# The first four token tiles loaded in two halves, the planner's tie rule and starting times for VectorE and GpSimd changed, and a new order of operations

## The chip, the core and the metric

The kernel runs on one core of a Trainium2 chip. A time is the device time of one execution in microseconds (us). Three executions of the kernel before took 198.56, 198.58 and 199.02 us; their median, 198.58 us, is the time that the change is measured against.

## The reference

A transformer block on x of 2048 tokens by 512 channels, all in bf16, with one conditioning vector c (512) that gives six modulation vectors. The first half is linear attention with 32 heads of 16 channels; the second is a gated feed-forward network with 1376 hidden units.

```python
mod = (_silu(c) @ w_mod)                       # sa, ca, ga, sb, cb, gb
h = _layernorm(x) * (1 + ca) + sa
q, k, v = split(h @ wqkv)                      # 32 heads of 16
pq, pk = q @ w_phi, k @ w_phi                  # per head
phi = concat(softmax(p), softmax(-p))          # for q and for k
kv, z = phi_k^T v, sum(phi_k)
o = (phi_q kv) / (phi_q z + 1e-6)
x = x + ga * (o @ wo)
h = _layernorm(x) * (1 + cb) + sb
x = x + gb * ((silu(h @ w_gate) * (h @ w_up)) @ w_down)
```

## The kernel before, in words

Tokens are worked on in 16 tiles of 128; four tiles are a chunk (`x_c0` to `x_c3` in the rows). Every weight is loaded into SBUF once. The work of a tile goes in this order. First the layer norm: VectorE takes statistics (`st`, `ln_mv`), ScalarE or GpSimd forms the reciprocal deviation, one of three engines writes the normalised tile `xn`. Then `xn` is turned (by TensorE for the first tiles, by a transposing DMA into `raw` for the later ones) and modulated into `hT`. TensorE multiplies it into keys (line 705), values (709) and queries (803). ScalarE takes exponentials (`e`, `eq`), VectorE sums them (`S`, `Sq`), and GpSimd or VectorE scales half of them (lines 774 and 827). The products of keys and values are summed over all tiles in the PSUM tile `kv_ps` (line 780). After the sixteenth tile VectorE makes `KVZ` from it. Then each query tile, turned into `pT` by a DMA, is multiplied with it (line 951), divided into `o`, turned into `oT`, multiplied with `wo` (line 984) and added to x. A second layer norm follows, then gate and up products (line 1044, and line 1090 for the last 96 hidden units), silu on ScalarE, a product on VectorE or GpSimd (`gu`), and the down projection (line 1122).

Before any key can be computed the program prepares two weights. `w_phi` (`wphi_sb`) becomes a block matrix `BD` (16 short matmuls in line 571, then GpSimd). The key weight `wk` is turned by TensorE (16 transposes in line 600 into four PSUM banks), copied to `WT512` (line 604), multiplied with `BD` (line 611, four matmuls a bank) and cast back into `wk` (line 614). Between these stand the products of c with `w_mod` (line 547), whose result `modA` is needed for the first `hT` (line 652).

The order of all operations is written out as a table. `ORDER` holds some 940 numbers: a number divided by four names an operation, the remainder chooses the engine among its alternatives. Each engine's queue is that list with the other engines' operations left out, so the order on each engine and the buffers that an operation gets come from `ORDER` alone. The planner's `run` walks these queues with a table of costs. Its times decide two things only: in what order the operations are written into the program, and how many filler matmuls (line 1196: products of a constant tile with itself, whose result nobody uses) `fill` puts in front of a TensorE operation that the plan expects to start late. Filler was put in ahead of the first key matmul only. An operation with the mark `DVE*` is a VectorE operation from SBUF to SBUF; the plan lets such an operation and a GpSimd operation exclude each other in time. `Buf(at=...)` tells the plan from when a loaded buffer may be read. Where two candidates may start at the same time, the plan takes the one for which the second value is smaller:

```python
if best is None or (t, not o.star) < best[:2]:
    best = t, not o.star, o
```

All transposing DMAs and nearly all loads and stores are issued by SyncE (SP) in the order of the table, each waiting there until what it reads is ready.

Of the kernel before, what the change touches and what calls it, by code (L numbers as in the profile page):

```python
# [20 lines left out]
D = 512  # L21
KD = D // P
# [13 lines left out]
def fm_size(m):  # L36
# [84 lines left out]
class Plan:  # L121
# [67 lines left out]
    def run(self, fill):  # L189
# [4 lines left out]
        for _ in self.ops:  # L194
            best = None
            for e, q in queue.items():
                if head[e] == len(q):
                    continue
                o = q[head[e]]
# [10 lines left out]
                if best is None or (t, not o.star) < best[:2]:  # L210
                    best = t, not o.star, o
# [33 lines left out]
def kernel(  # L245
# [128 lines left out]


    bx = [Buf() for _ in range(NT)]
    bwk, bwv, bwq = [Buf()] * KD, Buf(), [Buf()] * KD
    bm1, bm2 = [Buf() for _ in range(KD)], [Buf(), Buf()]
    bwo = [Buf() for _ in range(KD)]
    bwd = [Buf() for _ in range(FM)]  # L380
# [855 lines left out]
```

## Time and profile before

| | us |
|---|---|
| median of three executions | 198.58 |
| the profiled execution | 198.82 |
| its span, first to last instruction | 197.0 |
| TensorE busy in the span | 189.3 |
| VectorE busy | 131.6 |
| ScalarE busy | 114.2 |
| GpSimd busy | 113.4 |

The profiled execution is 0.24 us above the median; 1.82 us of it lie outside the span. TensorE is busy for 96% of the span, in every slice of the page except the first and the last with at least eight tenths. Busy time of TensorE includes filler and matmuls at the lower clock, so the share alone does not say what is left to gain.

### The profile page before, as it was taken

The numbers are of one execution on the slowest core, as the hardware profiler recorded it, in microseconds if no ns is written. First come the engines' busy times: TensorE is split into PE (matmuls) and PEld (weight loads), VectorE is DVE, ScalarE is ACT, GpSimd is POOL, SyncE is SP. The second block draws the span as 40 slices with busy tenths as digits, with TensorE's granted clock in tenths as the row PEclk, the third lists the DMA queues.
The fourth block names the chain that finished last, engine by engine and source line by source line (L and its number), as shares of the span: only waits on it lengthen the run. The fifth ranks groups of instructions, "written<-read, shape, count | busy, mean of one in ns | idle before, by whom it ended". The sixth has DMA issues, their size and how long they took to land.

```text
span 197.0 us, 3999 instructions
## 1 busy us (share of the span) xinstructions
PE 189.3 (96%) x1455; PEld 107.3 (54%) x1479; DVE 131.6 (67%) x262; ACT 114.2 (58%) x259; POOL 113.4 (58%) x184
## 2 busy tenths in 40 slices
PE   5989999999999999999999999999999999999993
PEld 2755555544655867977655455444444444454442
DVE  4899999999999989989857636531322620242453
ACT  2699999998899973873962775542322325430000
POOL 1658999999696976765581736745204424240510
DMA  5998994999948894937976431210000010100222
GB/s 195 389 372 117 170 344 129 223 391 232 278 118 156 77 195 78 161 68 113 191 92 131 84 80 46 61 36 0 13 3 13 0 53 0 53 5 13 80 82 67
DMA packets 51142, 24.17 MB, mean 123 GB/s; under 512 B 42449, under 2 KB 47922, under 8 KB 51122
## 3 DMA queue, kind: packets, MB, share of 16 engines
q1 hardware_dynamic: 50832, 23.86, 51.3%
q8 instruction: 11, 0.18, 0.4%
q10 hardware_dynamic: 290, 0.05, 0.1%
q14 instruction: 9, 0.07, 0.1%
HBM read 11.58 MB, written 2.10 MB: 69 GB/s over the span
## 4 chain that ended last, share of the span: by engine, by line
PE 83%; DVE 6%; POOL 4%; DMA 3%; issue 2%; DVEq 0%; POOLq 0%
PE one_ps L1044 34%; PE one_ps L1122 17%; PE one_ps L984 7%; PE one_ps L803 6%; PE one_ps L705 4%; PE one_ps L709 4%; PE one_ps L1090 3%; DVE st L404 2%; DMA wphi_sb<-in_A_w_phi_dram 2%; PE kv_ps L951 2%; PE kv_ps L780 2%; POOL e L774 2%; POOL xn L473 2%; DVE Sq L811 1%; DMA out_dram<-ot 1%
## 5 line engine op out<-in xcount | busy, mean ns | idle before, releaser
L1044 PE MATMUL one_ps<-hT,wgu_sb 128*128 128x512 bf16 (+2 forms) x475 | 73.6, 307 | 0.3
L1044 PEld LDWEIGHTS <-wgu_sb 128*128 128x128 bf16 x480 | 40.4, 98 | 28.9
L1060 POOL TENSOR_TENSOR gu<-usb,sg 128x512 bf16<-128x512 bf16 x19 | 21.9, 1155 | 36.2 <-ACT usb L1058 18.8
L1051 ACT ACTIVATE sg<-one_ps 128x512 bf16<-128x512 f32 (+1 forms) x41 | 23.2, 588 | 30.4 <-PE one_ps L1044 25.9
L1122 PE MATMUL one_ps<-wd_sb,gu 128*128 128x512 bf16 (+1 forms) x155 | 37.2, 372 | 0.2
L1054 DVE TENSOR_TENSOR gu<-one_ps,sg 128x512 bf16<-128x512 f32 (+1 forms) x22 | 14.2, 654 | 19.7 <-PE one_ps L1044 13.9
L1132 DVE TENSOR_TENSOR fg<-one_ps,gab 128x512 bf16<-128x512 f32 (+1 forms) x16 | 10.6, 669 | 24.2 <-PE one_ps L1122 24.2
L1122 PEld LDWEIGHTS <-gu 128*128 128x128 bf16 x180 | 16.7, 98 | 17.2
L811 DVE TENSOR_REDUCE Sq<-eq 128x64 f32<-128x1024 bf16 x16 | 19.3, 1208 | 0.0
L728 DVE TENSOR_REDUCE S<-e 128x64 f32<-128x1024 bf16 x16 | 18.6, 1207 | 0.2 <-ACT e L720 0.2
L720 ACT ACTIVATE e<-one_ps 128x512 bf16<-128x512 f32 x32 | 16.8, 603 | 0.9 <-PE one_ps L705 0.9
L807 ACT ACTIVATE eq<-one_ps 128x512 bf16<-128x512 f32 x32 | 16.9, 603 | 0.7 <-PE one_ps L803 0.5
L1058 ACT CAST usb<-one_ps 128x512 bf16<-128x512 f32 x19 | 11.0, 584 | 9.7 <-PE one_ps L1044 8.3
L984 PE MATMUL one_ps<-wo_sb,oT 128*128 128x512 bf16 x58 | 15.2, 379 | 0.6 <-DVE gul L1097 0.3
L705 PE MATMUL one_ps<-wk,hT 128*128 128x512 bf16 x62 | 15.0, 379 | 0.7 <-ACT hT L652 0.6
L803 PE MATMUL one_ps<-wq,hT 128*128 128x512 bf16 x63 | 15.4, 379 | 0.1
L709 PE MATMUL one_ps<-wv,hT 128*128 128x512 bf16 x60 | 15.2, 379 | 0.1
L774 POOL TENSOR_TENSOR e<-e,rho 128x512 bf16<-128x512 bf16 x14 | 14.5, 1050 | 0.2
L995 DVE SCALAR_TENSOR_TENSOR x_c<-one_ps,x_c 128x512 bf16<-128x512 f32 x14 | 9.4, 679 | 6.1 <-PE one_ps L984 6.0
L827 POOL TENSOR_TENSOR eq<-eq,Rq 128x512 bf16<-128x512 bf16 x12 | 12.5, 1048 | 0.5
L404 DVE BATCH_NORM_STATS2 st<-x_c 128x6 f32<-128x512 bf16 x17 | 11.0, 679 | 1.8 <-DMA x_c<-in_A_x_dram 1.8
L998 ACT ACTIVATE xn<-x_c 128x512 bf16<-128x512 bf16 x14 | 8.7, 627 | 5.9 <-DMA raw<-xn 3.2
(138 smaller groups left out, 274.1 us busy)
## 6 DMA issues: line engine op xcount, KB each, us to landing
wmod_sb<-in_w_mod_dram SPq DMA_DIRECT2D x2, 1024.0 KB, 7.3
out_dram<-ot SPq DMA_DIRECT2D x15, 128.0 KB, 1.9
x_c<-in_A_x_dram SPq DMA_DIRECT2D x3, 512.0 KB, 6.7
wgu_sb<-in_B_w_up_dram SPq DMA_DIRECT2D x1, 1376.0 KB, 7.2
wgu_sb<-in_B_w_gate_dram SPq DMA_DIRECT2D x1, 1376.0 KB, 12.0
wd_sb<-in_B_w_down_dram SPq DMA_DIRECT2D x1, 1280.0 KB, 7.2
wk<-in_A_wqkv_dram SPq DMA_DIRECT2D x1, 512.0 KB, 4.7
wmod_sb<-in_w_mod_dram SPq DMA_DIRECT2D x1, 512.0 KB, 6.0
```

Of the source, the lines that this page charges most:

```text
L705: nc.tensor.matmul(pk()[:], lhsT=hT[c_i][k][:, cols], rhs=Wk2[:, k, :], start=(k == 0), stop=(k == KD - 1))
L709: nc.tensor.matmul(v()[:], lhsT=hT[c_i][k][:, cols], rhs=wv_sb[:, k, :], start=(k == 0), stop=(k == KD - 1))
L728: pl.op("DVE", r=[e], w=([Ss] if y == 0 else []) + [parts[y]], us=1.13, fn=lambda: nc.vector.tensor_reduce(Ss()[:, y].rearrange("p g (s h) ...
L774: eng.tensor_tensor(e()[:, :, 1], e()[:, :, 1], rho()[:, y].unsqueeze(2).to_broadcast([P, G, DH, 4]), op=ALU.mult)
L803: nc.tensor.matmul(pq()[:], lhsT=hT[c_i][k][:, cols], rhs=Wq2[:, k, :], start=(k == 0), stop=(k == KD - 1))
L807: pl.op("ACT", r=[pq, btab], w=[be[sg]], us=0.48, fn=lambda sg=sg: nc.scalar.activation(eq[:, :, sg].rearrange("p g f h -> p g (f h)"), pq ...
L811: pl.op("DVE", r=be, w=[Sq], us=1.13, fn=lambda: nc.vector.tensor_reduce(Sq()[:].rearrange("p g s h -> p (g s) h"), eq[:].rearrange("p g s ...
L984: nc.tensor.matmul(a()[:], lhsT=oT()[:, j0 + j, :], rhs=wo_sb[:, j, :], start=(j == 0), stop=(j == KD - 1))
L1044: nc.tensor.matmul(ps_()[0:fsz, q * n:(q + 1) * n], lhsT=wgu_sb[:, k, i, m * P:m * P + fsz], rhs=h2[k], start=(k == 0), stop=(k == KD - 1))
L1051: pl.op("ACT", r=[g, btab], w=[sg], us=0.08 + 0.41 * L / CW, fn=lambda: nc.scalar.activation(sg()[0:fsz, 0:L], g()[0:fsz, 0:L], ACT.Silu))
L1060: pl.op("POOL", r=[usb, sg], w=[gu], us=0.17 + 0.98 * L / CW, fn=lambda: nc.gpsimd.tensor_tensor(gu()[0:fsz, 0:L], usb()[0:fsz, 0:L], sg() ...
L1122: nc.tensor.matmul(fp()[:], lhsT=b()[0:fsz, c0:c0 + P], rhs=wd_[0:fsz, m, wcs], start=(m == 0), stop=(m == FM - 1))
```

## The change

The first four tiles of x are loaded in two transfers of two tiles (256 KB each) instead of one of 512 KB. The plan is told that `w_phi` can be read from 4.7 us (3.4 before) and `wk` from 6.3 us (0 before), and that some transfers count for slightly more or fewer bytes. On a tie the plan now takes the engine, VectorE or GpSimd, whose last exclusive operation ended earlier. `ORDER` is a new list. No other line differs; the line numbers of the program after are higher by one or two.

```diff
 ORDER = [
-    0, 4, 72, 56, 60, 65, 80, 8, 12, 76, 85, 128, 120, 132, 124, 88, 94, 44, 48, 52, 216, ...
+    60, 0, 76, 72, 84, 80, 88, 4, 132, 65, 124, 48, 52, 136, 128, 140, 92, 8, 236, 241, 56, ...
...
-                if best is None or (t, not o.star) < best[:2]:
-                    best = t, not o.star, o
+                late = o.star != (pool >= star)
+                if best is None or (t, late) < best[:2]:
+                    best = t, late, o
...
-    bwk, bwv, bwq = [Buf()] * KD, Buf(), [Buf()] * KD
+    bwk, bwv, bwq = [Buf(at=6.3)] * KD, Buf(), [Buf()] * KD
...
-    bc, bphi = Buf(at=5.5), Buf(at=3.4)
+    bc, bphi = Buf(at=5.5), Buf(at=4.7)
...
-    later(x_ch[0][:], x_v[0], bx[0:4], 480)
-    later(Wk2[:], wqkv_v[:, :, D:2 * D], bwk[0:1], 640)
-    for k, n, kb in ((0, 2, 660), (2, 1, 270), (3, 1, 260)):
+    for t in (0, 2):
+        later(x_ch[0][:, t:t + 2, :], x_v[0][:, t:t + 2, :], bx[t:t + 2], 278)
+    later(Wk2[:], wqkv_v[:, :, D:2 * D], bwk[0:1], 556)
+    for k, n, kb in ((0, 2, 665), (2, 1, 252), (3, 1, 256)):
...
-    later(wv_sb[:], wqkv_v[:, :, 2 * D:3 * D], [bwv], 560)
+    later(wv_sb[:], wqkv_v[:, :, 2 * D:3 * D], [bwv], 500)
```

The new table gives some operations to another engine. The counts, before and after, are: scalings of `eq` on VectorE 4 and 1, on GpSimd 12 and 15; second-norm writes of `xn` on VectorE 5 and 1, the others on ScalarE and GpSimd; copies to `WT512` on VectorE 2 and 3, on ScalarE 2 and 1; the small copy of `phs` on ScalarE before and on VectorE after; the first pair's reciprocal deviation on GpSimd before and on ScalarE after. TensorE has the same work in both, apart from filler.

The first place is the head of TensorE's queue. These are its rows in the program before where the filler ends and the 16 short matmuls on `wphi_sb` begin; five fillers of 512 columns stand ahead of them, and three more of 512 follow them.

```order
L1196 LDWEIGHTS ones_101
L1196 MATMUL kv_ps_72<-ones_101 128x512
L571 LDWEIGHTS WT0_98
L571 MATMUL one_ps0_73<-wphi_sb_89,WT0_98 128x16
```

In the program after, the same place reads as below; eight fillers of 512 columns and one of 154 stand ahead of it, and a single one of 449 columns stands between the four short matmuls on `c_row` and the transposes of `wk`.

```order
L1198 MATMUL kv_ps_72<-ones_101 128x512
L1198 LDWEIGHTS ones_101
L1198 MATMUL kv_ps_72<-ones_101 128x154
L573 LDWEIGHTS WT0_98
L573 MATMUL one_ps0_73<-wphi_sb_89,WT0_98 128x16
```

Filler has moved from behind the short matmuls to ahead of them. The two fillers of 512 columns and one of 312 ahead of the first key matmul are in both programs.

The second place is VectorE's queue after the statistics of the first two tiles; `st61` and `st62` are the statistics of the third and fourth. Before:

```order
L404 BN_STATS st62_258<-x_c0_79 128x6
L405 BN_AGGR ln1_mv2_183<-st61_246 128x2
L405 BN_AGGR ln1_mv2_183<-st62_258 128x2
L459 TENSOR_REDUCE ln1_0_nmr_181<-ln1_mv0_179 128x2
L534 TENSOR_TENSOR silucT_136<-sig_134,one_ps1_74 128x4
L467 TENSOR_SCALAR xn0_282<-x_c0_79,ln1_mv0_179,ln1_0_nmr_181 128x512
L604 COPY WT512_186<-one_ps5_78 128x4x128
L604 COPY WT512_186<-one_ps4_77 128x4x128
L459 TENSOR_REDUCE ln1_2_nmr_184<-ln1_mv2_183 128x2
L467 TENSOR_SCALAR xn1_322<-x_c0_79,ln1_mv2_183,ln1_2_nmr_184 128x512 x2
L552 COPY modA_137<-one_ps1_74 128x8
```

And after, from the third tile's statistics on:

```order
L579 COPY phs_143<-one_ps0_73 128x64
L405 BN_STATS st62_255<-x_c0_79 128x6
L406 BN_AGGR ln1_mv2_183<-st61_244 128x2
L406 BN_AGGR ln1_mv2_183<-st62_255 128x2
L460 TENSOR_REDUCE ln1_0_nmr_181<-ln1_mv0_179 128x2
L606 COPY WT512_186<-one_ps2_75 128x4x128
L536 TENSOR_TENSOR silucT_136<-sig_134,one_ps1_74 128x4
L606 COPY WT512_186<-one_ps3_76 128x4x128
L460 TENSOR_REDUCE ln1_2_nmr_184<-ln1_mv2_183 128x2
L606 COPY WT512_186<-one_ps5_78 128x4x128
L468 TENSOR_SCALAR xn1_319<-x_c0_79,ln1_mv2_183,ln1_2_nmr_184 128x512
L468 TENSOR_SCALAR xn0_281<-x_c0_79,ln1_mv0_179,ln1_0_nmr_181 128x512
```

The copies of the turned `wk` now stand ahead of all three writes of `xn`, and there are three of them.

The third place is SP's queue where the attention of the first pairs of tiles is turned: `eq` into `pT` for the query tiles, `o` into `oT` for the product with `wo`. Before:

```order
L831 DMA_TRANSPOSE pT1_857<-eq1_161 128x8x128
L974 DMA_TRANSPOSE oT0_1080<-o0_1050 128x8x128
L831 DMA_TRANSPOSE pT2_918<-eq6_166 128x8x128
L831 DMA_TRANSPOSE pT3_1047<-eq7_167 128x8x128
L831 DMA_TRANSPOSE pT0_841<-eq9_169 128x8x128
L1006 DMA_TRANSPOSE raw0_1332<-xn21_1231 128x8x128
```

After:

```order
L833 DMA_TRANSPOSE pT0_918<-eq1_161 128x8x128
L833 DMA_TRANSPOSE pT2_952<-eq6_166 128x8x128
L833 DMA_TRANSPOSE pT3_1050<-eq7_167 128x8x128
L833 DMA_TRANSPOSE pT1_934<-eq9_169 128x8x128
L976 DMA_TRANSPOSE oT1_1128<-o0_1052 128x8x128
L1008 DMA_TRANSPOSE raw0_1344<-xn21_1241 128x8x128
L1101 DMA_TRANSPOSE gut0_1368<-gul0_126 128x1x128
L833 DMA_TRANSPOSE pT0_918<-eq8_168 128x8x128
L976 DMA_TRANSPOSE oT0_1093<-o1_1084 128x8x128
L332 DMA wd_sb_88<-in_B_w_down_dram 96x512
```

The second pair's `oT` has moved behind three `pT`, and the load of the last 96 rows of `w_down`, which before stood right behind the second half of `w_mod` early in the queue, now stands behind the third pair's `oT`.

## Rows read from the trace of the kernel before

**Rows 1.** Waits of TensorE from 12.3 to 190 us: engine, line, releaser, sums

```profile
PE one_ps L705 <- ACT hT L652: 0.6, 1, 0.6
PE one_ps L984 <- DVE gul L1097: 0.3, 1, 0.3
```

**Rows 2.** Timeline of TensorE, the first 13 us: start, length, operation, idle before

```profile
1.44 2.31 PE L1196 MATMUL kv_ps<-ones 128*128 128x512 bf16 x5 [1.44 <-DVE ones L338]
4.65 0.57 PE L571 MATMUL one_ps<-wphi_sb,WT 128*128 128x16 bf16 x16 [0.90 <-DMA wphi_sb<-in_A_w_phi_dram]
5.08 1.44 PE L1196 MATMUL kv_ps<-ones 128*128 128x512 bf16 x3
...
6.64 1.69 PE L600 MATMUL one_ps<-ident_b,wk 128*128 128x128 bf16 x16
8.17 0.39 PE L611 MATMUL one_ps<-BD,WT 128*128 128x128 bf16 x4
...
10.08 1.05 PE L649 MATMUL one_ps<-ident_b,xn 128*128 128x128 bf16 x16
...
12.28 3.20 PE L705 MATMUL one_ps<-wk,hT 128*128 128x512 bf16 x14 [0.58 <-ACT hT L652]
```

**Rows 3.** Timeline of VectorE, 4.3 to 10.5 us

```profile
4.41 0.69 DVE L404 BATCH_NORM_STATS2 st<-x_c 128x6 f32<-128x512 bf16 x1 [1.75 <-DMA x_c<-in_A_x_dram]
...
7.80 0.16 DVE L459 TENSOR_REDUCE ln_nmr<-ln_mv 128x2 f32<-128x4 f32 x1 [0.44 <-POOL ln_mv L457]
...
8.37 0.76 DVE L604 COPY WT<-one_ps 128x512 bf16<-128x512 bf16 x2
...
9.22 0.73 DVE L467 TENSOR_SCALAR xn<-x_c,ln_mv,ln_nmr 128x512 bf16<-128x512 bf16 x2
```

**Rows 4.** Timeline of ScalarE, 5 to 13.6 us

```profile
8.85 2.02 ACT L614 CAST wk<-one_ps 128x512 bf16<-128x512 f32 x4
10.74 2.82 ACT L652 ACTIVATE hT<-one_ps,modA 128x512 bf16<-128x512 bf16 x4
```

**Rows 5.** Tile `wk`, first 16 us: its load from issue to landing

```profile
DMA to landing us min/median/max: 4.7/4.7/4.7
```

**Rows 6.** Timeline of SP's queue, the issue of the load of `wk`

```profile
1.18 0.41 SPq L331 DMA_DIRECT2D wk<-in_A_wqkv_dram  x1
```

**Rows 7.** Engines in the second 5 us; last three: clock, DMA share, GB/s

```profile
5.00:10.00 5.00, 5.00 (x78) 3.75 (x75) 4.45 (x16) 3.30 (x11) 3.02 (x5) 1.00 1.06 390
```

**Rows 8.** Groups by shape: busy, mean ns, the scaling of `eq` by engine

```profile
L827 POOL TENSOR_TENSOR eq<-eq,Rq 128x512 bf16<-128x512 bf16 x12 | 12.5, 1048 | 0.5
...
L827 DVE TENSOR_TENSOR eq<-eq,Rq 128x512 bf16<-128x512 bf16 x4 | 2.0, 505 | 0.0
```

**Rows 9.** Timeline of TensorE, 66 to 72.5 us

```profile
66.39 3.29 PE L1044 MATMUL one_ps<-hT,wgu_sb 128*128 128x128 bf16 x56
69.99 1.90 PE L984 MATMUL one_ps<-wo_sb,oT 128*128 128x512 bf16 x7 [0.31 <-DVE gul L1097]
```

**Rows 10.** Tile `oT`, 50 to 90 us: its transposing DMAs from issue to landing

```profile
DMA to landing us min/median/max: 3.0/3.7/4.9
```

**Rows 11.** Timeline of SP's queue, 60 to 100 us

```profile
66.36 4.86 SPq L831 DMA_TRANSPOSE pT<-eq  x3
...
74.10 4.93 SPq L831 DMA_TRANSPOSE pT<-eq  x2
```

**Rows 12.** Timeline of GpSimd, 50 to 66 us: the two idle times

```profile
60.90 0.25 POOL L822 TENSOR_TENSOR Rq<-Rs,Sq 128x32 bf16<-128x32 f32 x1 [0.88 <-ACT Rs L816]
61.91 0.23 POOL L415 TENSOR_SCALAR ln_neg<-ln 128x1 f32<-128x1 f32 x1 [0.77 <-DVE ln L405]
```

**Rows 13.** Tile `wd_sb`: its two loads from issue to landing

```profile
DMA to landing us min/median/max: 7.2/8.0/8.7
```

**Rows 14.** Timeline of TensorE, 72 to 82 us

```profile
77.07 0.38 PE L1122 MATMUL one_ps<-wd_sb,gut 96*128 96x512 bf16 x1
...
77.95 2.78 PE L1044 MATMUL one_ps<-hT,wgu_sb 128*128 128x256 bf16 x24
```

78 rows, old and new, of the table ORDER are left out of this document.

## The prediction

> **What bounds the kernel now.** I read the waits of TensorE first, because its busy share of 96% in the table may hide waiting. From 12.3 us to the end it waits twice, 0.58 us ahead of the first key matmul and 0.31 us ahead of a product with `wo` [rows 1]. Everything else between 12.28 us and the last down projection is one unbroken queue of matmuls, and both programs hold the same ones. So the other engines, full as they are until about 70 us, set the time only where they make TensorE wait. What the change can take away is what lies ahead of the first key matmul, and the pause of 0.31 us. What it can add is a new wait anywhere.
>
> I then read TensorE's first 13 us [rows 2]. Five fillers, a pause of 0.90 us until `wphi_sb` has landed, 16 short matmuls, three fillers, the transposes of `wk` at 6.64, folding from 8.17, transposes of `xn` at 10.08, keys at 12.28. A filler of 512 columns takes (2.31 - 1.44) / 2 = 0.435 us, and the 16 transposes of `wk` start 1.53 us before the fold, 0.096 us apiece: that is the 1.2 GHz level. The 16 transposes of `xn` take 1.05 us with their last one's end; less the same tail (1.69 - 1.53 = 0.16) they take 0.89, 0.056 apiece, the 2.4 GHz level. So the clock rose at about 8.1 us, 6.7 us after the first filler and 3.5 us after the pause.
>
> VectorE waits 1.75 us for x, then has its chain of statistics, with one idle time of 0.44 us for GpSimd's reciprocal deviation, two copies at 8.37 and the last `xn` done at 9.95 [rows 3]. ScalarE casts `wk` from 8.85, 0.68 us after the first fold, and writes `hT` from 10.74; the keys follow 1.54 us later [rows 4].
>
> **The change, part by part: the head.** Filler first: 8 x 512 + 154 columns make 8.3 fillers, 3.61 us, so the short matmuls start at 1.44 + 3.61 = 5.05 instead of 4.65. They take 5.08 - 4.65 = 0.43, the `c_row` matmuls what is left of 6.64 - 5.08 after three fillers, 0.25, and the one filler of 449 columns 0.38: the transposes of `wk` could start at 6.11. `wk` landed at 1.18 + 4.7 = 5.88 [rows 5, 6]; its issue is now one issue of 0.41 us later, so it lands between 5.88 (the data bound it) and 6.29 (the issue bound it). I take a start of 6.2, 0.44 us earlier than before. At the low clock the fold starts 1.53 us later, at 7.73, also 0.44 us earlier. ScalarE's casts and `hT` follow it by the same distances, as ScalarE has one copy less to make: keys at 11.84.
>
> VectorE must keep up. Half of x is 0.262 MB; at the 390 GB/s that the queue moved in the second 5 us [rows 7] it lands 0.67 us earlier, at 3.74. From first statistics to last `xn` VectorE took 9.95 - 4.41 = 5.54, of which 0.44 idle; now that wait should go, because the deviation is made by ScalarE early, and one copy (0.38) and the small `phs` copy (estimated at 0.2, half a copy) are added: 5.68, so `xn` is done at 9.42, 0.53 us earlier. That is just ahead of the fold's gain, so TensorE's chain decides: -0.44 at the low clock.
>
> The pause of 0.90 us goes away, and TensorE then works without a break from 1.44 us. If the clock rises before the transposes, they take 0.89 instead of 1.53, and `xn` becomes the bound: transposes of `xn` at 9.5, and keys 0.58 us earlier. I take -0.5 for the head. If the half of x lands no earlier than the whole did, `xn` is done at 4.41 + 5.68 = 10.09, and the head gains nothing. Bounds: 0 and -0.6.
>
> The rule in the Trainium skill's page "TensorE: Matmul & The Clock Gate" (Part 1: The HAM clock gate) is that the array's clock is throttled by default and that activity releases it. By it the unbroken filler should bring the rise forward, and the head would gain 0.58; the rows show only that filler with a pause behind it did not do so.
>
> **The pause at 69.68.** The eight products with `wo` of the second pair start at 69.99 after 0.31 us of waiting [rows 9]. Their `oT` now stands behind three `pT` in SP's queue, and in TensorE's queue it stands behind 16 more gate and up matmuls (56 take 3.29, so 0.9), four more products with `wo` (half of 1.90, so 0.9), 16 attention matmuls and four transposes (estimated at 0.7 together): 2.5 us. So it is wanted at 69.68 + 2.5 - 0.5 = 71.7. The three `pT` ended at 66.36 + 4.86 = 71.2 [rows 11]. If they keep their places but for the head, `oT` is issued at 70.7 and lands at the median of 3.7 us [rows 10] at 74.4: a wait of 2.7. But GpSimd, which feeds them, was idle for 0.88 and 0.77 us just ahead of them, waiting for ScalarE and VectorE [rows 12]; in the new order the scaling of `eq6` goes ahead of the second of these waits, and no `oT` stands ahead of the `pT` (some 1.3 us, about what a `pT` takes of the 4.86, less its waits). That makes 70.7 - 1.65 - 1.3 = 67.75, a landing at 71.45, and no wait. I stay near this end and take -0.2; bounds -0.31 and +2.7.
>
> **The late load.** The last 96 rows of `w_down` are now loaded behind the third pair's `oT`. In the kernel before, SP's place behind `eq8` is at about 75.4 [rows 11]; one more `oT` (1.3) less 0.7 for the earlier start gives an issue at 76. They are wanted by the short product at 77.07 [rows 14], which now has 24 gate and up matmuls (2.78 less a tail, 2.6) and some 0.8 us of smaller ones ahead of it: at 77.07 + 3.4 - 0.7 = 79.8. With a landing like the other small transfers of that stretch, 3.7 [rows 10], it arrives at 79.7, just in time; with the 8.7 of its own row [rows 13], at 84.7, a wait of 4.9. In that row two transfers of `w_mod` lay ahead of it; there is none now. I take 0, as the nearer row is the one of the same stretch; bounds 0 and +4.9.
>
> **What I cost at nothing.** The engines' other swaps, among them three scalings of `eq` from VectorE at 505 ns to GpSimd at 1048 [rows 8], and the rule for ties, which decides only how the program is written out and how much filler it holds. What hides them is TensorE's queue of ready matmuls. Where it runs dry, such a swap costs up to 0.54 us. The tail behind the last matmul has the same instructions in both.
>
> **Sum.** -0.5 - 0.2 = -0.7 on 198.82 of the profiled execution gives 198.12; that execution stood 0.24 above the median, so on the scale of the runs 197.9 us.
>
> **Rivals.**
> - *The halves bring nothing.* The Trainium skill's page "DMA: Bandwidth & Descriptors" (Bandwidth) advises transfers of 1 MiB and more and gives small ones a lower share of peak; by it two pieces of 256 KB would move slower than one of 512 KB, and what is queued behind them would land later. As a mechanism here: the first half lands with the second at 4.41, `wk` 0.41 us later, VectorE is last, and the head gains 0: 198.4 with the pause shortened, 198.6 without. Against it stand the 390 GB/s of rows 7, with 256 KB pieces of `w_mod` in that queue.
> - *`oT` becomes the wait* (the other side). If GpSimd does not get to `eq9` earlier, TensorE stands for up to 2.7 us at 71.7: 198.58 - 0.5 + 2.7 = 200.8. It decides against the change from a wait of 1.1 us on, which is an issue of `oT` later than 69.1. For it speaks that SP's queue is strictly in order; against it, the idle times of rows 12.
> - *The load of `w_down` comes late*: up to 198.58 - 0.7 + 4.9 = 202.8; it cancels the gain from a landing of 4.4 us on.
> - *Small new waits in the new order*, of 0.3 to 1 us in sum at places that I have not traced between 20 and 110 us: 198.2 to 198.9.
>
> **How the numbers follow.** The forecast, 197.6 to 198.1 us, gets 0.45; the halves that bring nothing 0.17; small new waits 0.20; the `oT` wait 0.12; the late load 0.06. A measurement of this kernel can tell about 0.3%, 0.6 us, from no change. Faster by more: most of the forecast, and a little that I have not foreseen, 0.45. Slower by more: the two waits, 0.18, and the end of the small ones, in all 0.20. Within it 0.35. The range for 8 times in 10 runs from 197.3 (head at -0.6, pause gone, and a few tenths that I do not see) to 199.2 (an `oT` wait of 1.2).
>
> **What would show it.** In the changed trace the first statistics should start near 3.75, the transposes of `wk` near 6.2, `xn` should be done near 9.4 and the keys start at 11.7 to 11.85. Gaps of 0.056 us between the transposes of `wk` would mean that the clock rose early. At 71.7 the products with `wo` should follow without a wait, and so should the 96-row product near 80. I am wrong if TensorE's waits behind the first key matmul sum to more than 1 us, or if `xn` or the transposes of `wk` do not start earlier.

## The result: slower, where faster was forecast

The changed kernel takes 200.3 us (median of five executions, 199.71 to 201.36), the kernel before 198.9 us over five (198.56 to 199.27). The ratio is 1.0076 with a 95% interval of 1.0053 to 1.0098: slower, outside the range given. The profiled execution took 199.91 us with a span of 198.1, so 1.1 us more than that of before. Of two experiments below, e11_wk_act and e14_halves_sg, the profiled execution was slower than the others, and the ratios leave it out.

I read the waits of TensorE again first, from 5 us to the end. They answer to [rows 1]; the columns are the same.

```profile
PE one_ps L602 <- DMA wk<-in_A_wqkv_dram: 1.6, 1, 1.6
PE one_ps L1046 <- ACT sg L1053: 0.4, 1, 0.4
```

Both waits of before are gone and two others have come. The larger one is for the load of `wk`. TensorE's first 13 us show it; they answer to [rows 2].

```profile
1.44 3.38 PE L1198 MATMUL kv_ps<-ones 128*128 128x512 bf16 x9 [1.44 <-DVE ones L339]
4.65 0.55 PE L573 MATMUL one_ps<-wphi_sb,WT 128*128 128x16 bf16 x16
...
5.31 0.36 PE L1198 MATMUL kv_ps<-ones 128*128 128x449 bf16 x1
7.32 1.53 PE L602 MATMUL one_ps<-ident_b,wk 128*128 128x128 bf16 x16 [1.64 <-DMA wk<-in_A_wqkv_dram]
8.64 0.63 PE L613 MATMUL one_ps<-BD,WT 128*128 128x128 bf16 x4
...
11.46 1.05 PE L651 MATMUL one_ps<-ident_b,xn 128*128 128x128 bf16 x16
...
12.91 3.29 PE L707 MATMUL one_ps<-wk,hT 128*128 128x512 bf16 x13
```

The filler is unbroken, as intended, and ends at 5.67. Then TensorE stands for 1.64 us. The transposes of `wk` start at 7.32 instead of 6.64, the keys at 12.91 instead of 12.28. The 14 key matmuls also have small stops between them, because `hT` is closer behind. So the better mark for the head is what follows them, the transposes of the next `xn`. They start at 16.32; in the trace of the kernel before they stand here:

```profile
15.31 0.61 PE L489 MATMUL one_ps<-ident_b,xn 128*128 128x128 bf16 x8
```

By this mark the head lost 1.01 us. The tile `wk`, first 16 us, says from when to when it was loaded; [rows 5, 6] had 4.7 us from the issue at 1.18.

```profile
DMA to landing us min/median/max: 5.6/5.6/5.6
```

The issue is at 1.64, the landing at 7.27. The stretches of 1 us of the changed kernel show how slowly (columns: TensorE, its weight loads, VectorE, ScalarE, GpSimd; then the granted clock, the DMA share, GB/s):

```profile
4.00:5.00 1.00, 1.00 (x18) 0.64 (x17) 1.00 (x2) 0.00 (x0) 0.00 (x0) 1.00 0.78 228
5.00:6.00 1.00, 0.68 (x14) 0.36 (x10) 0.96 (x6) 0.50 (x3) 0.00 (x0) 1.00 0.71 219
6.00:7.00 1.00, 0.00 (x0) 0.00 (x0) 0.93 (x5) 0.64 (x5) 0.84 (x2) 1.00 0.96 318
7.00:8.00 1.00, 0.68 (x10) 0.69 (x11) 0.25 (x1) 0.43 (x2) 1.00 (x2) 0.87 1.03 389
8.00:9.00 1.00, 1.00 (x12) 1.00 (x10) 0.75 (x5) 0.54 (x1) 0.10 (x1) 0.50 1.05 402
...
11.00:12.00 1.00, 1.00 (x28) 1.00 (x27) 0.37 (x2) 1.00 (x3) 0.00 (x0) 0.92 1.03 381
```

The first two of these stretches in the kernel before:

```profile
4.00:5.00 1.00, 0.35 (x13) 0.34 (x13) 0.59 (x1) 0.00 (x0) 0.00 (x0) 1.00 1.08 378
5.00:6.00 1.00, 1.00 (x12) 0.34 (x8) 0.97 (x5) 0.21 (x1) 0.43 (x1) 1.00 1.08 366
```

The DMA engines moved 228 and 219 GB/s where they had moved 378 and 366, and were busy for 0.71 to 0.78 of the time although issued loads had not landed. The clock is the second thing to see: TensorE stood still from 5.67 to 7.32, and the granted clock falls between 7 and 8 us and is 0.50, the 1.2 GHz level, until just after 11. The second wait of TensorE, 0.45 us at 92.75, is new. It is read with e7_sg_first.

The sum closes at the last matmul, which starts 1.20 us later (194.81 against 193.61): +1.01 at the head, -0.31 for the wait of [rows 9], +0.45 for the new one; 0.05 is left over.

### The profile page after: what moved, and what is told of

Its sections match the earlier page's. It is cut to its first block, busy times and chain, and to the rows that moved or that the text cites. A ratio compares the mean times of both kernels' runs of the same rounds, so it can differ in the third digit from the quotient of the medians.

```text
span 198.1 us, 3999 instructions
## 1 busy us (share of the span) xinstructions
PE 190.2 (96%) x1458; PEld 108.0 (55%) x1481; DVE 128.3 (65%) x260; ACT 117.0 (59%) x262; POOL 113.8 (57%) x183
## 4 chain that ended last, share of the span: by engine, by line
PE 88%; DMA 6%; issue 1%; ACT 1%; DVE 1%; SPq 0%; DVEq 0%; ACTq 0%
PE one_ps L1046 33%; PE one_ps L1124 17%; PE one_ps L805 7%; PE one_ps L711 7%; PE one_ps L707 7%; PE one_ps L986 6%; DMA wk<-in_A_wqkv_dram 3%; PE one_ps L1092 3%; DMA raw<-xn 2%; PE kv_ps L782 2%; PE kv_ps L953 2%; PE one_ps L613 1%; DMA out_dram<-ot 1%; PE one_ps L549 1%; PE one_ps L602 1%
## 5 line engine op out<-in xcount | busy, mean ns | idle before, releaser
L1124 PE MATMUL one_ps<-wd_sb,gu 128*128 128x512 bf16 (+1 forms) x154 | 36.7, 372 | 0.3
L829 POOL TENSOR_TENSOR eq<-eq,Rq 128x512 bf16<-128x512 bf16 x15 | 15.8, 1051 | 1.9 <-DVE Rq L825 1.4
L776 POOL TENSOR_TENSOR e<-e,rho 128x512 bf16<-128x512 bf16 x13 | 13.5, 1049 | 0.2
L1138 POOL TENSOR_TENSOR ot<-x_c,fg 128x512 bf16<-128x512 bf16 (+1 forms) x5 | 5.3, 1056 | 11.7 <-DMA out_dram<-ot 7.7
```

The source lines that it names most:

```text
L1124: nc.tensor.matmul(fp()[:], lhsT=b()[0:fsz, c0:c0 + P], rhs=wd_[0:fsz, m, wcs], start=(m == 0), stop=(m == FM - 1))
```

## The experiments

Each ratio is against executions of the kernel before that were taken along with it. "wk" is when the first and the last of the 16 parts of its load landed (the trace has an event for each; the time between them is called the spread below), "mark" the start of the transposes behind the first 14 key matmuls.

| kernel | ratio, 95% interval | wk, us | mark, us |
|---|---|---|---|
| before | 1 | 5.50 to 5.86 | 15.31 |
| after | 1.0076, 1.0053 to 1.0098 | 5.55 to 7.27 | 16.32 |
| e1_one_x | 0.9972, 0.9955 to 0.9990 | 5.27 to 5.69 | 14.70 |
| e2_halves_only | 1.0077, 1.0050 to 1.0105 | 5.57 to 7.57 | 18.76 |
| e3_wk_between | 1.0030, 0.9988 to 1.0071 | 5.02 to 6.30 | 17.10 |
| e4_fill | 1.0082, 1.0057 to 1.0106 | 5.44 to 6.39 | 15.98 |
| e5_small_between | 1.0039, 1.0009 to 1.0069 | 5.38 to 7.10 | 15.13 |
| e6_by_rows | 1.0110, 1.0068 to 1.0151 | 6.58 to 7.06 | 18.17 |
| e7_sg_first | 0.9952, 0.9932 to 0.9971 | 5.45 to 5.84 | 14.82 |
| e8_filler_only | 1.0000, 0.9974 to 1.0026 | 5.32 to 5.71 | 15.20 |
| e9_small_first | 0.9995, 0.9972 to 1.0018 | 5.59 to 6.33 | 15.14 |
| e10_phs_act | 0.9940, 0.9919 to 0.9962 | 5.31 to 5.64 | 14.80 |
| e11_wk_act | 0.9933, 0.9912 to 0.9953 | | |
| e12_both | 1.0291, 1.0241 to 1.0340 | 7.64 to 11.01 | 20.74 |
| e13_more_ahead | 1.0155, 1.0113 to 1.0198 | 6.30 to 8.44 | 18.64 |
| e14_halves_sg | 1.0035, 1.0011 to 1.0059 | | |

Theory H: the halves make `wk` land late. Its rival O: something else at the head does, or chance.

**e1_one_x**, the change without the halves. The empty operation keeps the numbers of `ORDER`. Extra filler that the plan would add behind the transposes of `wk` is held back, so that the filler stays as in the change but for 22 columns ahead of the keys; the same is done in e3, e5 to e7 and e9 to e13.

```diff
-    for t in (0, 2):
-        later(x_ch[0][:, t:t + 2, :], x_v[0][:, t:t + 2, :], bx[t:t + 2], 278)
+    later(x_ch[0][:], x_v[0], bx[0:4], 480)
+    pl.op("XBAR", us=0.0, kb=1, fn=lambda: None)
```

> The changed kernel with the first four tiles of x again in one transfer, all else (order, filler, tie rule) as in the change. Theory H (the halves are what made the load of wk land late, at 7.3 us instead of 5.9): wk lands near 5.9, TensorE does not wait for it, the statistics start at 4.4, the last xn is done near 10.1 and the keys start near 12.3. That returns the 1.0 us that the head lost: 198.8 to 199.1 us, within 0.2 us of the kernel before. Theory O (the late landing belongs to something else that the change did to the head, or to chance): wk lands after 7 us again, keys start near 12.9, and the time stays near 200.

Measured: 198.66 us, faster than the kernel before. TensorE's timeline of e1_one_x, then VectorE's first statistics and last `xn`:

```profile
6.08 1.71 PE L602 MATMUL one_ps<-ident_b,wk 128*128 128x128 bf16 x16
7.82 0.38 PE L613 MATMUL one_ps<-BD,WT 128*128 128x128 bf16 x4
...
9.73 1.05 PE L651 MATMUL one_ps<-ident_b,xn 128*128 128x128 bf16 x16
...
11.19 0.38 PE L707 MATMUL one_ps<-wk,hT 128*128 128x512 bf16 x1
```

```profile
4.23 0.69 DVE L405 BATCH_NORM_STATS2 st<-x_c 128x6 f32<-128x512 bf16 x1 [1.58 <-DMA x_c<-in_A_x_dram]
...
8.40 1.05 DVE L468 TENSOR_SCALAR xn<-x_c,ln_mv,ln_nmr 128x512 bf16<-128x512 bf16 x3
```

No wait for `wk`, and no fall of the clock once it had risen, at about 7.4 us (the starts of these transposes are 0.107 us apart until then and 0.056 after). The keys start at 11.19, 1.1 us earlier than I expected here: I had kept the late `xn` of 10.09 from the prediction, but VectorE was done with `xn` at 9.45 with x whole. H holds, and the rest of the change is worth 0.6 us at the mark.

**e2_halves_only**, the kernel before with the halves alone.

```diff
-    later(x_ch[0][:], x_v[0], bx[0:4], 480)
+    pl.op("XBAR", w=bx[0:4], us=0.5, kb=480, fn=lambda: [
+        nc.sync.dma_start(x_ch[0][:, t:t + 2, :], x_v[0][:, t:t + 2, :]) for t in (0, 2)])
```

> The kernel before, with nothing but the first load of x cut into two halves. H: wk lands near 7.3 us, TensorE waits for it behind the c_row products for some 0.6 us, the keys start between 12.8 and 13.3, and the kernel takes 199.2 to 199.9. O: wk lands by 6.3 at the latest, the transposes of wk start at 6.64 as before, the keys at 12.3 or a little earlier, and the time is that of the kernel before within 0.3 us.

Measured: 200.66 us, and the same late landing. TensorE's timeline of e2_halves_only:

```profile
7.62 1.89 PE L601 MATMUL one_ps<-ident_b,wk 128*128 128x128 bf16 x16 [1.78 <-DMA wk<-in_A_wqkv_dram]
...
12.14 1.87 PE L650 MATMUL one_ps<-ident_b,xn 128*128 128x128 bf16 x16
```

The loss is larger than expected. The trace is of the slowest of its eight executions, 202.49 us, so its mark may overstate the usual loss: there the transposes of `xn` take 1.87 us instead of the 1.05 of [rows 2], as TensorE worked at the lower level until past 16 us.

**e3_wk_between**, `wk` issued between the halves (4 and 8 are the second half of x and `wk` in the table).

```diff
-    60, 0, 76, 72, 84, 80, 88, 4, 132, 65, 124, 48, 52, 136, 128, 140, 92, 8, 236, ...
+    60, 0, 76, 72, 84, 80, 88, 8, 132, 65, 124, 48, 52, 136, 128, 140, 92, 4, 236, ...
```

> The changed kernel with the load of wk issued between the two halves of x, as the second transfer. If wk is late because it is issued third (0.46 us later) and its rows are then fetched slowly, it lands by 5.7 here, the second half of x by 6.3, TensorE does not wait for wk, and VectorE is the last: xn near 10.3 us, keys at 12.0 to 12.4, 198.8 to 199.2 us. If any transfer that follows a 256 KB piece is fetched slowly, wk still takes 5.6 us from its issue, lands near 6.8, and TensorE waits for it for about 1.1 us: 199.4 to 199.9.

Measured: 200.96 us, from 198.66 to 201.87, and unclear against the kernel before. `wk`, issued second and at 1.18 us, landed at 6.30, 5.1 us after its issue, its parts 1.28 us apart; neither forecast fits. TensorE then waited elsewhere, for `BD`, 1.22 us at 9.14, because VectorE copies `phs` behind the late statistics.

**e4_fill**, the changed kernel with filler over the wait.

```diff
             left = int((o.start - t0) * 1250 if t0 < 7.0 else (o.start - t0 - 0.2) * 1400)
+            if 5.5 < t0 < 6.2 and left >= 128:
+                left += 4500
```

> The changed kernel with 4500 more columns of filler ahead of the transposes of wk, about 1.9 us at the higher clock, so that TensorE works while it waits for wk. If the clock, which fell to 0.5 at 7.7 us after TensorE had stood still from 5.7 to 7.3, is a good part of the loss: no row at 0.5, the transposes of wk at 7.55, 0.056 us apart, folds from 8.45, keys near 12.2 without small stops, and 0.5 to 0.9 us of the head's 1.0 us comes back: 199.0 to 199.4. If only the late landing counts: keys at 12.9 as in the changed kernel, and 199.9 or more.

TensorE's timeline of e4_fill:

```profile
5.70 2.64 PE L1198 MATMUL kv_ps<-ones 128*128 128x512 bf16 x10
8.18 1.06 PE L602 MATMUL one_ps<-ident_b,wk 128*128 128x128 bf16 x16
```

Measured: 201.04 us. The granted clock did not fall, and the 16 transposes take 1.06 us instead of 1.53. From their start to the mark it is 7.80 us (15.98 - 8.18), in the changed kernel 9.00 (16.32 - 7.32): some 1.2 us for the clock. But the filler held the transposes until 8.18 while `wk` had landed at 6.39 this time, and 1.4 us of new stops follow at 31 to 34 and 78 us, so the kernel is no faster. The mechanism is right, the remedy is not.

**e5_small_between**: as e1_one_x, with a 1 KB load between x and `wk`.

```diff
-    pl.op("XBAR", us=0.0, kb=1, fn=lambda: None)
+    pl.op("XBAR", us=0.0, kb=1, fn=lambda: nc.sync.dma_start(wd_sb[0:1, 0, :], c[:, :]))
```

> The changed kernel with x in one transfer, as in e1_one_x, and a load of 1 KB put between x and wk on SP's queue, so that wk is issued third, 0.46 us later, as behind the halves. If it is the later issue that spreads the landings of wk: its 16 parts land over more than 1 us, the last after 6.8, TensorE waits for wk, and the time is 199.5 or more. If it is the cutting of x: the parts land within 0.6 us of each other, the last by 6.3, the keys start at 11.2 to 11.6, and the time is that of e1_one_x, 198.3 to 198.9.

Waits of TensorE, its transposes, and the tile `wk`, of e5_small_between:

```profile
PE one_ps L602 <- DMA wk<-in_A_wqkv_dram: 1.1, 1, 1.1
```

```profile
7.14 1.07 PE L602 MATMUL one_ps<-ident_b,wk 128*128 128x128 bf16 x16 [1.10 <-DMA wk<-in_A_wqkv_dram]
```

```profile
DMA to landing us min/median/max: 5.5/5.5/5.5
```

Measured: 199.64 us. A load of 1 KB ahead of `wk` spreads its parts as the halves do, over 1.72 us. So it is not the cutting of x as such. The cost is less, 1.0039 against 1.0076: in this trace the 1.10 us of waiting did not take the clock back, the transposes ran at the higher level, 2.4 GHz (0.056 us apart), and from their start to the mark it is 7.99 us (15.13 - 7.14), near the 7.80 of e4_fill.

**e6_by_rows** cuts x by partitions, in rows of 4 KB.

```diff
-    later(x_ch[0][:], x_v[0], bx[0:4], 480)
+    pl.op("XBAR", w=bx[0:4], us=0.5, kb=480, fn=lambda: [
+        nc.sync.dma_start(x_ch[0][p:p + 64], x_v[0][p:p + 64]) for p in (0, 64)])
+    pl.op("XBAR", us=0.0, kb=1, fn=lambda: None)
```

> The changed kernel with the first load of x cut the other way: two transfers of 64 partitions with 4 KB each, instead of two of 128 partitions with 2 KB each. Both pieces have 256 KB, and wk is issued third. If the pieces of 2 KB make the difference: wk's parts land within 0.6 us of each other, the last by 6.3, and the time is 198.3 to 199.0. If any two transfers ahead of wk do it: the last part lands after 6.8 us, TensorE waits, 199.5 or more.

Measured: 201.56 us. `wk` is third here too, but its parts lie within 0.48 us. It is late for another reason: x itself took until 5.53, as it loads more slowly in pieces of 64 partitions. The stretch of e6_by_rows in which x was still loading:

```profile
4.00:5.00 1.00, 1.00 (x5) 0.45 (x4) 0.00 (x0) 0.00 (x0) 0.00 (x0) 1.00 0.98 203
```

The DMA engines were busy there (0.98), unlike in the changed kernel (0.78).

**e9_small_first**: the 1 KB load ahead of x.

```diff
+    pl.op("XBAR", us=0.0, kb=1, fn=lambda: nc.sync.dma_start(wd_sb[0:1, 0, :], c[:, :]))
     later(x_ch[0][:], x_v[0], bx[0:4], 480)
-    pl.op("XBAR", us=0.0, kb=1, fn=lambda: None)
```

> As e5_small_between, but the load of 1 KB stands ahead of x, so wk is third on SP's queue and issued near 1.6 us again, while x is issued 0.4 us later too and holds the DMA engines until about 4.7. If the parts of wk spread because it is the third transfer, or because it is issued at 1.6: spread over 1 us, the last landing after 7 us. If they spread when the engines come to wk too soon after its issue (its 64th packet started 2.2 to 2.5 us behind the issue in the kernels with a spread of 0.95 to 2.0, and 2.6 to 2.8 behind it in those with 0.36 to 0.48): the 64th packet near 4.3, 2.7 us behind the issue, a spread under 0.6, and the last landing near 6.3. The time then lies 0 to 0.5 us above e1_one_x.

Measured: 199.01 us, a spread of 0.74, the last part at 6.33. That is between the two forecasts and nearer to the second.

**e13_more_ahead**: 256 KB in place of the 1 KB (and 109 columns more filler); the rest of that chunk of x stays at its later place.

```diff
-    pl.op("XBAR", us=0.0, kb=1, fn=lambda: None)
+    later(x_ch[1][:, 0:2, :], x_v[1][:, 0:2, :], bx[TPC:TPC + 2], 265)
...
```

> As e5_small_between, but in place of the 1 KB load it is the first half of the next chunk of x, 256 KB, that stands between x and wk. wk is third and issued at 1.6 us in both. If the parts of wk spread because it is third, or because it is issued at 1.6: they spread over more than 1 us, the last lands after 7.5 us. If they spread when the DMA engines are through with what stands ahead too soon after the issue: the engines come to wk at 4.4 or later, at least 2.8 us behind its issue, its parts land within 0.5 us of each other, the last by 6.7, and the keys start 0.5 to 0.8 us later than in e1_one_x.

Measured: 202.25 us. The stretches of e13_more_ahead, and its tile `wk`:

```profile
4.00:5.00 1.00, 1.00 (x5) 0.45 (x4) 0.90 (x2) 0.00 (x0) 0.00 (x0) 1.00 0.42 134
5.00:6.00 1.00, 1.00 (x23) 0.76 (x20) 0.96 (x4) 0.23 (x1) 0.00 (x0) 1.00 0.63 184
```

```profile
DMA to landing us min/median/max: 6.8/6.8/6.8
```

My theory of the time between the issue and the engines' coming falls. They came to `wk` at 5.15 (its 64th packet), 3.5 us after the issue, and the parts spread over 2.14 us all the same. That it is third falls with e6_by_rows. What fits all twelve kernels with `wk` on SP's queue and x in 128 partitions is only a description: with the whole of x straight ahead of it the parts lie within 0.33 to 0.74 us, with 256 KB in rows of 2 KB or with 1 KB straight ahead within 0.95 to 2.14. It is one of `wk` alone: the second half of x, right behind the first, landed within 0.73 us in the changed kernel (3.73 to 4.46). Nor does the idling of the DMA engines go with every spread: in e3_wk_between and e4_fill their share from 4 to 6 us was 0.92 or more, and the parts still lay 1.28 and 0.95 us apart. What the engines are waiting for where they idle stays open.

**e8_filler_only**: the kernel before with the new filler (more that the plan would add behind the transposes of `wk` is held back).

```diff
-    bwk, bwv, bwq = [Buf()] * KD, Buf(), [Buf()] * KD
+    bwk, bwv, bwq = [Buf(at=6.3)] * KD, Buf(), [Buf()] * KD
-    bc, bphi = Buf(at=5.5), Buf(at=3.4)
+    bc, bphi = Buf(at=5.5), Buf(at=4.7)
```

> The kernel before, its order of operations kept and x in one transfer, with the filler of the change alone: 8 x 512 and 154 columns ahead of the products with wphi and 449 ahead of the transposes of wk, so without the pause of 0.90 us. If the 0.6 us that e1_one_x gained at the head came from the unbroken filler: the clock rises before 7.6 us, the transposes of wk start near 6.1, the folds near 7.8, the transposes of xn of the third pair near 14.8 instead of 15.31, and the time is 0.3 to 0.6 us under the kernel before. If it came from the new order on VectorE and ScalarE: xn is done at 9.95 as before, the keys start at 12.2, and the time is that of the kernel before.

Measured: 199.01 us, ratio 1.0000. TensorE's timeline of e8_filler_only:

```profile
5.94 1.06 PE L600 MATMUL one_ps<-ident_b,wk 128*128 128x128 bf16 x16
7.17 0.39 PE L611 MATMUL one_ps<-BD,WT 128*128 128x128 bf16 x4 [0.18 <-POOL BD L582]
8.48 0.16 PE L545 MATMUL one_ps<-zero_one,ones 1*128 1x8 bf16 x1 [0.91 <-DVE silucT L534]
```

The clock rose early and the folds came 1.0 us earlier than in [rows 2], and then TensorE waited for VectorE, whose `silucT` stood behind the wait of [rows 3] for GpSimd. The filler buys nothing without the new order, which has that deviation from ScalarE. The new order without the filler was not tried.

**e7_sg_first**: e1_one_x with one operation moved on ScalarE (2349 is the `hT`, 2188 and 2224 the two `sg`).

```diff
-    ... 2412, 2349, 2140, 2848, 1664, 1668, 1616, 2852, 2856, 2872, 2188, 2224, 1952, ...
+    ... 2412, 2140, 2848, 1664, 1668, 1616, 2852, 2856, 2872, 2188, 2224, 2349, 1952, ...
```

> The changed kernel with x in one transfer, as in e1_one_x, and on ScalarE the first hT of line 1017 that waits at 88.5 us for the landing of raw moved behind the two sg that stood behind it. If the 0.8 us that TensorE waits for sg at 91 us comes from that place in ScalarE's queue: the wait is gone, hT comes 0.4 us later and nobody waits for it, and the time is 0.5 to 0.8 us below e1_one_x, 197.8 to 198.2, under both kernels. If the wait only moves to the next operation in want of raw: within 0.2 us of e1_one_x.

ScalarE's timeline of the changed kernel, then of e7_sg_first:

```profile
91.62 0.60 ACT L1017 ACTIVATE hT<-raw,modB 128x256 bf16<-128x256 bf16 x1 [1.41 <-DMA raw<-xn]
92.12 1.06 ACT L1053 ACTIVATE sg<-one_ps 128x512 bf16<-128x512 f32 x2
```

```profile
89.14 1.06 ACT L1053 ACTIVATE sg<-one_ps 128x512 bf16<-128x512 f32 x2
90.72 0.60 ACT L1017 ACTIVATE hT<-raw,modB 128x256 bf16<-128x256 bf16 x1 [0.52 <-DMA raw<-xn]
```

Measured: 198.07 us. By the ratios that is 0.4 us under e1_one_x (0.9952 against 0.9972), and the two intervals overlap. The profiled executions of both took 198.63 us: in e7_sg_first the wait for `sg` is gone, but others have come, 0.96 us for `BD` and 0.43 us for `wv`. So the cause of the wait is shown, ScalarE standing in line for a transposing DMA with work behind it that was ready; its price is not sharp.

**e14_halves_sg** is the changed kernel with that same edit.

> The changed kernel, halves and all, with only the edit of e7_sg_first: on ScalarE the first hT of line 1017 that waits for raw moved behind two sg. The head is that of the changed kernel. If the late landing of wk belongs to the halves, its parts spread over 0.9 us or more again, the last lands after 6.3 us, and the time stays at least 1 us above e7_sg_first: 199.2 to 200.2. The edit itself should be worth the 0.4 us that TensorE waited for sg in the changed kernel. If the head of the changed kernel was an accident of its executions: 198.0 to 198.6.

The ratio of 1.0035 confirms that the halves keep the kernel slower than before even so. Between the kernels with and without them lie 0.0083 here (against e7_sg_first) and 0.0104 in the change (against e1_one_x), and in neither pair do the intervals overlap. The edit is worth 1.0076 - 1.0035, some 0.8 us; that is more than the 0.4 forecast, but the two intervals overlap.

**e10_phs_act**: e7_sg_first with the copy of `phs` on ScalarE, first in its queue.

```diff
-    60, 0, 76, 72, 84, 80, 88, 4, 132, 65, 124, ...
+    60, 64, 0, 76, 72, 84, 80, 88, 4, 132, 124, ...
```

> e7_sg_first with the small copy of phs on ScalarE again, as in the kernel before, ahead of everything else there. BD then is made from 5.3 us instead of 6.6 and TensorE's wait of 1.0 us for it is gone: folds from 7.1 instead of 7.9. If the folds set the head, the keys come 0.3 to 0.6 us earlier: 197.5 to 197.8. If the xn, which are done at 9.4 instead of 9.57, set it: 0.1 to 0.2 us, 197.8 to 198.1.

Measured: 197.88 us, ratio 0.9940. Against e7_sg_first the gain is not clear of noise. The folds start at 7.62, not 7.1: the wait for `BD` became one for `silucT` (0.80 us).

**e11_wk_act** and **e12_both** bring the halves back with `wk` on ScalarE's queue; e11 on e7_sg_first, ahead of `c_row`, e12 on e10_phs_act, behind it. The edit of e11_wk_act:

```diff
     nc.scalar.dma_start(wphi_sb[:], A_w_phi.rearrange("h (q t) f -> (h q) (t f)", t=4))
+    nc.scalar.dma_start(Wk2[:], wqkv_v[:, :, D:2 * D])
     nc.scalar.dma_start(c_row[:], c[:, :])
...
-    later(Wk2[:], wqkv_v[:, :, D:2 * D], bwk[0:1], 556)
+    pl.op("XBAR", w=bwk[0:1], us=0.0, kb=556, fn=lambda: None)
```

> e7_sg_first with x in two halves again, and wk issued by ScalarE between wphi and c_row at 1.16 us, on another queue than x. If the halves can help once wk doesn't stand behind them: first statistics near 3.9, wk landed by 6.0, xn done by 9.3, and 197.6 to 198.1. If the two queues share the engines so that x's halves land at 4.4 and later and wk after 6: no gain over e7_sg_first, or a loss of up to 1 us, 198.1 to 199.1.

> e10_phs_act with x in two halves again and wk issued by ScalarE on its own queue, now behind wphi and c_row, at 1.7 us. If the halves are good once wk doesn't stand behind them on x's queue: first statistics near 3.6, wk's last part by 6.2, xn done before 9.0, keys near 10.8, 197.2 to 197.6. If one or two of wk's parts land late all the same, as two of 16 did in the profiled execution of e11_wk_act (7.3 and 8.3 us, the others by 6.0): TensorE waits for wk, keys after 12, and 198.5 to 200.

e11_wk_act: five of its six executions took 197.53 to 197.84 us, ratio 0.9933, level with e10_phs_act. The sixth, of which the trace is, took 201.21: there `wk` landed between 5.42 and 8.29 us, and TensorE waited 3.00 us for `c_row`, which stands behind `wk` in that queue. So the gain did not come in every execution. e12_both missed by far, 204.76 us; the waits of TensorE in e12_both:

```profile
PE one_ps L603 <- DMA wk<-in_A_wqkv_dram: 4.8, 1, 4.8
```

`wk`, issued at 1.73 on the second queue, landed between 7.64 and 11.01 us. Between these two, the fastest and the slowest kernel here by their ratios, lie only the place of `wk` ahead of or behind a load of 1 KB and the copy of `phs`; which of the two spread the load further was not tried.

## Why the prediction was wrong

- **What bounds the kernel**: right. Behind the first key matmul the changed kernel has one wait of 0.45 us, and each kernel's time followed its head and its few waits.
- **The first half of x**: right. Statistics start at 3.80 (forecast 3.75).
- **The unbroken filler and the clock**: right as to mechanism, not as to the gain. In the changed kernel's trace the filler's starts are 0.427 us apart until 3.97 and 0.217 apart at its end; the short matmuls start at 4.65, not 5.05. That agrees with the Trainium skill, "TensorE: Matmul & The Clock Gate" (Part 1: The HAM clock gate), that activity releases the throttle. The moment is not set by the filler alone: in e1_one_x, with the same filler, the rise is at about 7.4 us, and its mark of 14.70 is no later than the 14.82 of e7_sg_first, whose transposes of `wk` all ran at the higher level. So an early rise is not what the head gained by. I had also priced only the rise: the pause that a late `wk` makes can take the clock back, for some 1.2 us by e4_fill. It does not in every execution: on record the mean granted clock is 1.0 in two of the five of the changed kernel (199.71 and 200.3 us) and 0.982 to 0.991 in three, while all five are slower than the five of the kernel before.
- **The step that failed** is in the head: "it lands between 5.88 (the data bound it) and 6.29 (the issue bound it)". It landed at 7.27. I moved the issue by 0.41 us and kept the rate, and did not ask whether the rate was still that of [rows 7] right behind a short transfer. "TensorE then works without a break from 1.44 us" fell with it: it stood for 1.64 us and then lost the clock. The head's -0.5 became +1.01.
- **The halves as a gain**: mis-sized, and hidden by luck. With `wk` on time and x whole (e1_one_x) the term is -0.61, the end of the bounds, and the ratio of 0.9972 is near the forecast (197.9 / 198.58 = 0.9966). But the forecast gave a whole x a head that gains nothing, as VectorE was to need 5.68 us from the first statistics to the last `xn`. It needed 5.22 (4.23 to 9.45), so the halves had nothing to bring there. In the changed kernel `xn` was done at 10.28, not 9.42, as the copies ahead of it wait for the late transposes.
- **The rival "the halves bring nothing"** had the right place, a later `wk`, but at worst no gain, where 1.01 us was lost. The rule of the Trainium skill on small transfers ("DMA: Bandwidth & Descriptors", Bandwidth) spoke against the change and was set aside because 256 KB pieces of `w_mod` ran at full rate in the same queue. They do here too (402 GB/s at 8 to 9 us). What is slow is the load of `wk` right behind a short transfer at the queue's start.
- **The pause at 69.68**: right. It is gone. `oT` is issued at 69.58 and lands at 72.80, and its eight products with `wo` follow at 73.13 without a wait, 0.33 us later. The forecast was an issue at 67.75, a landing at 71.45 and products at 71.7; as the head came out 1.5 us later than forecast, these stand for 69.25, 72.95 and 73.2.
- **The late load of `w_down`**: right, with little to spare. It was issued at 78.23, landed 2.7 us later, at 80.93, and the short product ran at 81.10 without a wait.
- **Small new waits**: came true as a rival, 0.45 us at 92.75, and e7_sg_first, where it is gone, shows its cause.

These two rows of the changed kernel, of SP's queue and of TensorE, answer to [rows 11] and [rows 9]:

```profile
69.58 1.25 SPq L976 DMA_TRANSPOSE oT<-o  x1
```

```profile
73.13 1.89 PE L986 MATMUL one_ps<-wo_sb,oT 128*128 128x512 bf16 x8
```

## What to carry to other kernels

A transfer that is cut so that its first piece comes early also changes what the next transfer stands behind, and when that one is on the critical path its landing is to be watched, part by part, not its average rate. A wait ahead of TensorE can cost twice, its own length and the clock that the pause takes back; it did in the changed kernel and did not in e5_small_between. When an in-order queue waits for a DMA, look for work behind it that was ready: one moved operation was worth 0.4 to 0.8 us here by the ratios, though not clear of noise.

## What was not expected of the hardware

- A load of 1 KB put ahead of a 512 KB load spread the 16 parts of the latter from 0.41 us (e1_one_x) to 1.72 us (e5_small_between), with the DMA share at 0.57 in the stretch from 5 to 6 us while transfers were queued. The Trainium skill, "DMA: Bandwidth & Descriptors" (Queues, rings and completion order), says that one copy is split over up to 16 rings; the 16 landing events agree. The parts are not in step: in the changed kernel packets of `w_mod`, issued after `wk`, start from 5.27 us on, while those of `wk` go on starting until 6.84. No run here shows what the idle engines waited for.
- The kernel before took 8.67 us from the transposes of `wk` to the mark (15.31 - 6.64), with the rise of the clock at about 8 us. The same order took 11.14 us in the trace of e2_halves_only (18.76 - 7.62), where TensorE had stood for 1.78 us ahead of the transposes and the rise came only past 16 us. In e5_small_between a stop of 1.10 us left the clock at the higher level.
- The granted clock of the first stretches reads 1.00 while filler of 512 columns takes 0.427 us there; the spacing tells more than that column until the first change is recorded.
